# Attention into a gated feed-forward, one core: the lower bound on the weights' bits moved from GpSimd to VectorE, with a new table of planned times

## The chip, the cores and the metric

One core of a Trainium2 chip runs the kernel in a single launch. The metric is the device time of the run in microseconds, lower is better. Before the change it is 532.01 us, the median of three runs (531.34 to 532.36).

## What is computed

Inputs `q`, `k`, `v` have the shape (8 batches, 8 heads, 576 positions, 64); the three weights arrive as 64-bit floats, a float32 drawing times a float64 factor each.

```python
rel = pos[:, None] - pos[None, :]
scores = np.where((rel >= 0) & (rel < 64), q @ k.T / 8, -1e9)
attn = exp(scores - max);  attn /= attn.sum() + 1e-09
x = (attn @ v)                        # heads laid side by side: (8, 576, 512)
h = np.maximum(x @ w_in, 0)           # 512 -> 1024
conv = conv_w[0]*h[s-1] + conv_w[1]*h[s] + conv_w[2]*h[s+1]
out = (h * sigmoid(conv)) @ w_out     # 1024 -> 512
```

## The kernel before

**Tiles.** The 4608 positions are worked through in 12 units of 384. In each unit there are four pairs of heads (c = 0 to 3), eight groups of 128 feed-forward features (f = 0 to 7) and four groups of 128 outputs (o = 0 to 3). A float32 factor is split into a rounded high part and a remainder, so that each product is three matmuls: high by high, low by high, high by low. So `mm1` (L498 to L502) issues 96 matmuls a unit and `mm2` (L558 to L564) another 96.

**Attention of a unit.** Three blocks of scores: `qk` (TensorE, L350), `row_max` (VectorE, L357, adds the mask and takes the row's extreme), `exps` (ScalarE, L367, with the row's sum), `guard` (adds 1e-9 to the sums, L370: on GpSimd in units 0 to 2, on VectorE later), `reciprocal` (L373) and `normalise` (L378). In units 0 and 1 the weights are transposed by TensorE (L384) and copied out by ScalarE (L389), later by VectorE (L405) and DMAs (L417). `values` (L481) multiplies with v; `split_hi` (ScalarE, L485) and `split_lo` (VectorE, L488) leave `xh` and `xl`, the two parts of the unit's input. Two units' worth of `xh` and `xl` exist, so attention runs one unit ahead.

**Feed-forward of a unit.** For each f: `mm1`, then `relu` (ScalarE, L522 or L518); for each pair of f: `conv_mid` (ScalarE, L528), `conv_side` (VectorE, L535, four instructions), `sig` (ScalarE, L542), `gate` (VectorE, L547), `gate_hi` (ScalarE, L551), `gate_lo` (VectorE, L555), and then `mm2`, whose sums the output copies (L600, L602) take.

**Weights.** They are turned to float32 on the chip, once, while units 0 and 1 run. `weights` (L258) does it in nine steps: `w_in` in two steps of 512 columns and three of 1024, `w_out` in four of 1024. A step has a load of the bits (SP, L264), then `to_f32` (L244): the absolute value of the upper word (ScalarE, L248), the lower bound TINY on it (GpSimd, L249), a shift and mask (VectorE, L250), the sign put in (VectorE, L252), the lower word scaled (ScalarE, L255) and added (VectorE, L256); then the rounded high part (GpSimd, L269) and the remainder (VectorE, L270). All go through two buffers of bits (tile `T`, `T_100` in the order rows) and two of results (tile `w`, there `w_101` and `w_102`). The 24 convolution weights take the same path without the split (`weights_conv`, L291; tile `cw`).

**What sets the order.** Each step is entered in a plan with a planned time, an engine, a planned cost and the names it reads and writes. `queued` (L61) plays the plan through: at each point it takes the engine that can start first and on it the ready work with the smallest planned time, and issues instructions in that order; the engines then run their queues in order. Planned times of units 0 and 1 and of the loads come from the table START (first two entries of its triples; the third is for all later units). SWITCH and LEAVE are planned costs of changing the kind of work; PORT_CL and `port` keep some VectorE and GpSimd works apart in the plan. Where the plan sees TensorE idle in the first 110 us, it puts in matmuls on a spare tile (`keep_busy`, L207): `n = int((start - t) * FILL)`. They keep the engine active and compute nothing that is used.

Of the kernel before, what the change touches and what calls it, by code (L numbers as in the profile page):

```python
# [8 lines left out]
F32 = mybir.dt.float32  # L9
# [3 lines left out]
ALU = mybir.AluOpType  # L13
# [20 lines left out]
TINY = 2.0 ** -15  # L34
# [26 lines left out]
def queued(works, fill=None):  # L61
# [30 lines left out]
    while left:  # L92
# [17 lines left out]
        if fill and e == "PE" and start < FILL_TO:  # L110
# [4 lines left out]
            if n > 0 and clean:  # L115
                order.append(Work(x.t, e, 0.0, fill(n, min(clean)[1]), [], [], None, 0, 0.0))
        turn = SWITCH[e] if e in SWITCH and (x.kind != state[e] if e == "PE" else x.kind and x.kind != state[e]) else 0.0
        if turn and e == "PE" and not x.kind:
            turn = LEAVE
        if e == "PE" or x.kind:  # L120
# [17 lines left out]


START = {  # L140
    "v0": -27.5,
    "pv0": -15.968,
    "conv": -37.437,
    "bits": ((-46.561, -47.419), (-44.383, -45.007)),
    "qk1": -43.011,
    "v1": -11.849,
    "qk2": -2.185,
    "qk0": (-91.154, -52.794, -48.024),
    "ex0": (-42.377, -37.771, -19.993),
    "sc1": (-20.012, -18.408, -14.041),  # L150
    "ex1": (-8.106, -4.046, -3.778),
    "mask": -0.529,
    "sig": ((3.087, 7.079, 8.764, 10.751), (3.178, 6.73, 5.945, 9.966), (4.046, 6.806, 8.285, 10.314)),
    "in": (-39.031, -37.38, -33.878, -12.682, -12.013),
    "out": (-11.963, -8.679, 1.926, 7.315),
# [3 lines left out]
}  # L159
SWITCH = {"PE": 0.14, "ACT": 1.28}  # L160
LEAVE = 0.24
PORT_CL = 0.5
WARM = 5.0
FILL, FILL_FROM, FILL_TO = 4.0, 2.0, 110.0

# [2 lines left out]
def attention_moe(ctx: ExitStack, tc: tile.TileContext, q, k, v, w_in, conv_w, w_out, out):  # L168
    nc = tc.nc
# [4 lines left out]
    def many(n, shape, dt, name, where=pool):  # L174
        return [where.tile(shape, dt, name=f"{name}{i}") for i in range(n)]
# [7 lines left out]
    mask = many(3, [P, P], F32, "mask")  # L183
# [13 lines left out]
    bits = [flat.bitcast(U32)[:, 4 * DM * i:4 * DM * (i + 1)].rearrange("p (e two) -> p e two", two=2) for i in range(2)]  # L197
# [20 lines left out]
    def at(t, eng, cost, do, r=(), w=(), kind=None, mb=0, port=0.0):  # L218

        plan.append(Work(t, eng, cost, do, list(r), list(w), kind, mb, port))  # L220

    def two(t, eng, cost, do, **kw):
        at(t, eng, cost, do, port=cost, **kw)
# [17 lines left out]

    def to_f32(t, n, st, x, kb, kt):  # L244

        lw, hw, xu = st[..., 0], st[..., 1], x.bitcast(U32)

        at(t, "ACT", 0.0009 * n + 0.2, lambda: nc.scalar.activation(x, hw.bitcast(F32), AF.Abs), r=kb, w=kt)  # L248
        at(t, "POOL", 0.0027 * n + 0.02, lambda: nc.gpsimd.tensor_scalar(x, x, TINY, None, op0=ALU.max), w=kt, port=PORT_CL)  # L249
        two(t, "DVE", 0.00052 * n + 0.06, lambda: nc.vector.tensor_scalar(  # L250
            xu, xu, 3, 0x3FFFFFF8, op0=ALU.logical_shift_left, op1=ALU.bitwise_and), w=kt)
        two(t, "DVE", 0.00104 * n + 0.07, lambda: nc.vector.scalar_tensor_tensor(  # L252
            xu, hw, 0xC0000000, xu, op0=ALU.bitwise_and, op1=ALU.bitwise_or), r=kb, w=kt)

        at(t, "ACT", 0.0009 * n + 0.2, lambda: nc.scalar.activation(lw, lw, AF.Copy, scale=2.0 ** -29), w=kb)  # L255
        two(t, "DVE", 0.00104 * n + 0.07, lambda: nc.vector.tensor_tensor(xu, xu, lw, ALU.add), r=kb, w=kt)  # L256

    def weights(t, src, fs, hi, lo, key, buf, halves):  # L258

        e = slice(halves[0] * DM, (halves[-1] + 1) * DM)  # L260
        st, x = bits[buf][:, e], w24[buf][:, e]
        kb, kt = [("bits", buf, a) for a in halves], [("w24", buf, a) for a in halves]
        for f, a, tl in zip(fs, halves, load_at(buf, halves, t)):
            at(tl, "SP", 0.7, lambda f=f, a=a: nc.sync.dma_start(  # L264
                bits[buf][:, a * DM:(a + 1) * DM], src[f].bitcast(U32).rearrange("p (e two) -> p e two", two=2)),
               w=[("bits", buf, a)], mb=0.52)
        n = len(fs) * DM
        to_f32(t, n, st, x, kb, kt)
        two(t, "POOL", 0.00127 * n, lambda: nc.gpsimd.tensor_copy(hi, x), r=kt, w=[f"{key}{f}h" for f in fs])  # L269
        two(t, "DVE", 0.00104 * n + 0.07, lambda: nc.vector.tensor_tensor(lo, x, hi.bitcast(F32), ALU.subtract),  # L270
           r=kt + [f"{key}{f}h" for f in fs], w=[f"{key}{f}l" for f in fs])

    freed = {}

    def load_at(buf, halves, t):

        ts = [freed.get((buf, a), START["bits"][buf][a]) for a in halves]
        for a in halves:
            freed[(buf, a)] = t + 0.01
        return ts  # L280

    def weights_in(t, fs, *where):
        f = slice(fs[0], fs[-1] + 1)
        weights(t, w_in, fs, wih[:, f].rearrange("p f c e -> p (f c e)"),
                wil[:, f].rearrange("p f c e -> p (f c e)"), "in", *where)

    def weights_out(t, fs, *where):
        f = slice(fs[0], fs[-1] + 1)
        weights(t, w_out, fs, woh[:, f].rearrange("p f e -> p (f e)"), wol[:, f].rearrange("p f e -> p (f e)"), "out", *where)

    def weights_conv(t_load, t):  # L291
        at(t_load, "SP", 0.7, lambda: nc.sync.dma_start(
            cbits, conv_w.bitcast(U32).rearrange("p (e two) -> p e two", two=2)), w=["cbits"], mb=0.03)
        to_f32(t, 3 * NF, cbits, cw.rearrange("p k f -> p (k f)"), ["cbits"], ["cw"])
# [436 lines left out]
```

## Time and profile before

| | |
|---|---|
| median of three runs | 532.01 us |
| the profiled execution | 531.34 us |
| its span, first to last instruction | 529.6 us |
| TensorE (PE) busy with matmuls | 518.5 us, 98% |
| VectorE (DVE) busy | 380.3 us, 72% |
| ScalarE (ACT) busy | 379.7 us, 72% |
| GpSimd (POOL) busy | 112.6 us, 21% |
| granted TensorE clock | full level (2.4 GHz) in all 40 slices |

The shares are means over two very different stretches. In the page's table of 40 slices (13.2 us each), VectorE stands at 8 or 9 tenths from the second slice to the seventh and at 5 to 7 later; GpSimd does most of its work in the first seven; TensorE stands at 9 tenths nearly everywhere, but in the first 76 us a part of that is the spare matmuls (210 records, 28.6 us).

### The profile page before, as it was taken

How to read it: one execution, taken by the hardware profiler on the slowest of the kernel's cores; microseconds unless marked ns; L12 is line 12 of the kernel's file. 1: busy time of each engine (PE TensorE's matmuls, PEld its weight loads, DVE VectorE, ACT ScalarE, POOL GpSimd, SP SyncE). 2: the span in 40 equal slices, each digit the busy share in tenths (PEclk: the TensorE clock that was granted, in tenths of full speed). 3: DMA queues.
4: the chain of work that ended last, by engine and by line, in shares of the span. 5: the costliest groups of instructions: out<-in, count | busy, mean ns of one | idle time of the engine just before them, and what ended most of it. 6: DMA issues, size and time to landing. Idle time of an engine off the chain costs nothing.

```text
span 529.6 us, 14836 instructions
## 1 busy us (share of the span) xinstructions
PE 518.5 (98%) x5826; PEld 499.8 (94%) x5826; DVE 380.3 (72%) x1084; ACT 379.7 (72%) x1011; POOL 112.6 (21%) x196
## 2 busy tenths in 40 slices
PE   9998999999999999999999999999999999999996
PEld 8887889999999999999999999999999999999996
DVE  3899999985858667767767767767767667655552
ACT  2997897579896696696697687687687687544542
POOL 6664467113131011021021021021021021000000
PEclk9999999999999999999999999999999999999999
DMA  8984660237292173183083074073073053010011
GB/s 284 365 296 136 208 231 1 60 109 248 76 325 72 58 256 83 42 291 77 21 297 77 16 253 122 21 285 105 13 264 120 17 152 104 16 61 0 2 60 62
DMA packets 29463, 69.98 MB, mean 132 GB/s; under 512 B 5713, under 2 KB 17617, under 8 KB 29393
## 3 DMA queue, kind: packets, MB, share of 16 engines
q1 hardware_dynamic: 29392, 69.03, 39.7%
q8 instruction: 46, 0.75, 0.6%
q14 instruction: 25, 0.20, 0.1%
HBM read 47.73 MB, written 9.47 MB: 108 GB/s over the span
## 4 chain that ended last, share of the span: by engine, by line
PE 85%; DVE 9%; DMA 1%; ACT 1%; issue 1%; SPq 1%; POOL 0%; DVEq 0%
PE po L564 39%; PE acc L501 36%; PE acc L481 6%; PE sc L350 5%; DVE c L535 1%; DVE w L252 1%; DMA T<-in_w_in_dram 1%; DVE s L357 1%; DVE w L256 1%; DVE wil L270 1%; ACT s L367 1%; SPq L234 1%; DVE xl L488 1%; DVE s L378 1%; DVE w L250 1%
## 5 line engine op out<-in xcount | busy, mean ns | idle before, releaser
L501 PE MATMUL acc<-xh,wih 128*128 128x384 f32 x384 | 131.5, 342 | 0.8 <-DVE xl L488 0.8
L564 PE MATMUL po<-gh,woh 128*128 128x386 f32 (+1 forms) x384 | 132.1, 344 | 0.0
L535 DVE SCALAR_TENSOR_TENSOR c<-hbuf,cw,c 128x386 f32<-128x386 f32 (+1 forms) x192 | 109.6, 623 | 30.7 <-ACT c L528 30.7
L564 PE MATMUL po<-gh,wol 128*128 128x386 f32 (+1 forms) x384 | 129.9, 338 | 0.0
L564 PE MATMUL po<-gl,woh 128*128 128x386 f32 (+1 forms) x384 | 129.7, 338 | 0.0
L501 PE MATMUL acc<-xh,wil 128*128 128x384 f32 x384 | 129.7, 338 | 0.0
L501 PE MATMUL acc<-xl,wih 128*128 128x384 f32 x384 | 129.7, 338 | 0.0
L367 ACT ACTIVATE s<-s,nm 128x96 f32<-128x96 f32 (+2 forms) x288 | 105.1, 367 | 5.2 <-DVE nm L357 4.9
L555 DVE TENSOR_TENSOR gl<-c,gh 128x772 fp32r<-128x772 f32 (+1 forms) x48 | 55.8, 1162 | 28.2 <-ACT gh L551 28.1
L501 PEld LDWEIGHTS acc<-xh,wih 128*128 128x128 f32 x384 | 72.1, 188 | 2.9 <-POOL sm L370 0.7
L564 PEld LDWEIGHTS po<-gh,woh 128*128 128x128 f32 x384 | 72.2, 188 | 2.6
L378 POOL TENSOR_TENSOR s<-s,r 128x768 f32<-128x768 f32 x27 | 39.7, 1472 | 163.5 <-DVE r L373 150.7
L547 DVE TENSOR_TENSOR c<-c,hbuf 128x772 f32<-128x772 f32 (+1 forms) x48 | 47.4, 987 | 36.9 <-ACT c L542 36.7
L564 PEld LDWEIGHTS po<-gl,woh 128*128 128x128 f32 x384 | 72.3, 188 | 0.0
L564 PEld LDWEIGHTS po<-gh,wol 128*128 128x128 f32 x384 | 72.3, 188 | 0.0
L501 PEld LDWEIGHTS acc<-xh,wil 128*128 128x128 f32 x384 | 72.2, 188 | 0.0
L501 PEld LDWEIGHTS acc<-xl,wih 128*128 128x128 f32 x384 | 72.1, 188 | 0.0
L522 ACT ACTIVATE hbuf<-acc 128x384 f32<-128x384 f32 x64 | 30.9, 486 | 45.8 <-PE acc L501 45.4
L542 ACT ACTIVATE c<-c 128x772 f32<-128x772 f32 (+1 forms) x48 | 40.7, 848 | 30.2 <-DVE c L535 29.9
L357 DVE CUSTOM_DVE_ANT_0 s<-sc,mask 128x96 f32<-128x96 f32 (+2 forms) x272 | 51.5, 254 | 9.7 <-POOL mask L321 5.7
L367 ACT ACTIVATION_READ_ACCUMULATOR s<-s,nm 128x1 f32 x288 | 54.3, 189 | 0.0
L511 POOL COPY hbuf<-hbuf 128x4 f32<-128x4 f32 x44 | 16.7, 379 | 176.3 <-DVE c L547 176.2
(64 smaller groups left out, 644.5 us busy)
## 6 DMA issues: line engine op xcount, KB each, us to landing
v<-in_v_dram SPq DMA_DIRECT2D x24, 768.0 KB, 7.2
ub<-T SPq DMA_DIRECT2D x240, 48.0 KB, 1.9
k<-in_k_dram SPq DMA_DIRECT2D x22, 448.0 KB, 4.9
q<-in_q_dram SPq DMA_DIRECT2D x22, 384.0 KB, 6.9
out_dram<-T SPq DMA_DIRECT2D x8, 772.0 KB, 4.2
T<-in_w_in_dram SPq DMA_DIRECT2D x8, 512.0 KB, 6.6
T<-in_w_out_dram SPq DMA_DIRECT2D x8, 512.0 KB, 4.2
out_dram<-T SPq DMA_DIRECT2D x3, 768.0 KB, 6.4
```

Of the source, the lines that this page charges most:

```text
L350: nc.tensor.matmul(banks_of(u, b)[h][r:r + rows, i * P + o:i * P + n], qs[hs, 2 * g + p, t:t + rows], ks[hs, 2 * g + p, t + o:t + n], star ...
L357: nc.vector.tensor_tensor_reduce(out=ss[b][:, i, h, o:n], in0=banks_of(u, b)[h][:, i * P + o:i * P + n], in1=mask[m][:, o:n], scale=-0.125 ...
L367: nc.scalar.activation(x, x, AF.Exp, bias=nms[b][:, e], scale=-1.0, accum_out=sms[b][:, e])
L378: on.tensor_tensor(sv, sv, rs[b].unsqueeze(2).broadcast_to([P, 2 * NB, n]), ALU.mult)
L481: nc.tensor.matmul(acc[bank(("v", u, c))][h * D:(h + 1) * D, t * W:(t + 1) * W], vs[:, c, t, h], ub[g][:, 2 * p:2 * p + 2, 2 * t + h], sta ...
L501: nc.tensor.matmul(acc[bank(("m", u, f))][:, :NX], w[:, f, c], x[u % 2][:, c], start=(c == 0 and j == 0), stop=(c == NC - 1 and j == 2))
L522: nc.scalar.activation(hbuf[:, f, o:o + NX], ps[:, :NX], AF.Relu)
L535: nc.vector.scalar_tensor_tensor(c, hbuf[:, f, e:e + n], cw[:, e, f:f + 1], c, op0=ALU.mult, op1=ALU.add)
L542: nc.scalar.activation(c, c, AF.Sigmoid)
L547: nc.vector.tensor_tensor(c, c, hbuf[:, 2 * i:2 * i + 2, 1:1 + n], ALU.mult)
L555: nc.vector.tensor_tensor(gls[ring(u, i)][:, :, :n], cs[i % 2][:, :, :n], ghs[ring(u, i)][:, :, :n].bitcast(F32), ALU.subtract)
L564: nc.tensor.matmul(po[o][:, :n], w[:, f, es], x, start=(f == 0 and j == 0), stop=(f == NF - 1 and j == 2))
```

## The change

The lower bound of the nine weight steps becomes a VectorE instruction (`early=True`); that of the 24 convolution weights stays on GpSimd. The planned cost of the rounding copy is lowered from 0.00127 to 0.00104 us a column. Nearly all planned times of the loads and of units 0 and 1 are new, with SWITCH, LEAVE and PORT_CL; the third entries of the triples, which serve units from 2 on, are as they were. START in short (every number but those third entries is new):

```diff
 START = {
-    "conv": -37.437,
-    "bits": ((-46.561, -47.419), (-44.383, -45.007)),
+    "conv": -53.962,
+    "bits": ((-41.879, -47.051), (-42.277, -36.159)),
...
-SWITCH = {"PE": 0.14, "ACT": 1.28}
-LEAVE = 0.24
-PORT_CL = 0.5
+SWITCH = {"PE": 0.12, "ACT": 1.28}
+LEAVE = 0.19
+PORT_CL = 0.87
...
-    def to_f32(t, n, st, x, kb, kt):
+    def to_f32(t, n, st, x, kb, kt, early=False):
...
-        at(t, "POOL", 0.0027 * n + 0.02, lambda: nc.gpsimd.tensor_scalar(x, x, TINY, None, op0=ALU.max), w=kt, port=PORT_CL)
+        if early:
+            two(t, "DVE", 0.00052 * n + 0.06, lambda: nc.vector.tensor_scalar(x, x, TINY, None, op0=ALU.max), w=kt)
+        else:
+            at(t, "POOL", 0.0027 * n + 0.02, lambda: nc.gpsimd.tensor_scalar(x, x, TINY, None, op0=ALU.max), w=kt, port=PORT_CL)
...
-        to_f32(t, n, st, x, kb, kt)
-        two(t, "POOL", 0.00127 * n, lambda: nc.gpsimd.tensor_copy(hi, x), r=kt, w=[f"{key}{f}h" for f in fs])
+        to_f32(t, n, st, x, kb, kt, True)
+        his, los = [f"{key}{f}h" for f in fs], [f"{key}{f}l" for f in fs]
+        two(t, "POOL", 0.00104 * n, lambda: nc.gpsimd.tensor_copy(hi, x), r=kt, w=his)
```

Line numbers of the changed kernel are three or four higher than those above (L250 is the new VectorE bound, L253 its shift and mask).

How the order moves, first on VectorE after the three blocks of row maxima of unit 0, up to the next block of them. Before:

```order
L250 TENSOR_SCALAR w_101<-w_101 128x512
L252 SCALAR_TENSOR_TENSOR w_101<-T,w_101 128x512
L373 RECIPROCAL r_89<-sm_86 128x8
L378 TENSOR_TENSOR s_80<-s_80,r_89 128x1024
L256 ISA w_101<-T,w_101 128x1024
L270 TENSOR_TENSOR wil<-w_101,wih 128x512
```

Now:

```order
L255 SCALAR_TENSOR_TENSOR cw<-cbits,cw 128x24
L250 TENSOR_SCALAR w_101<-w_101 128x512
L253 TENSOR_SCALAR w_101<-w_101 128x512
L255 SCALAR_TENSOR_TENSOR w_101<-T,w_101 128x512
L250 TENSOR_SCALAR w_101<-w_101 128x512
L376 RECIPROCAL r_89<-sm_86 128x8
L253 TENSOR_SCALAR w_101<-w_101 128x512
L381 TENSOR_TENSOR s_80<-s_80,r_89 128x1024
L255 SCALAR_TENSOR_TENSOR w_101<-T,w_101 128x512
L259 ISA w_101<-T,w_101 128x1024 x2
L274 TENSOR_TENSOR wil<-w_101,wih 128x512
```

Both 512-column steps now go through VectorE here, each with its own bound (L250), and the convolution weights are ahead of them.

GpSimd in the same place and after it, before:

```order
L249 TENSOR_SCALAR w_101<-w_101 128x512
L370 TENSOR_SCALAR sm_86<-sm_86 128x8
L269 CAST wih<-w_101 128x512
L370 TENSOR_SCALAR sm_87<-sm_87 128x8
L249 TENSOR_SCALAR w_101<-w_101 128x512
L249 TENSOR_SCALAR w_102<-w_102 128x1024
L433 MEMSET s_80 128x2x64
L269 CAST wih<-w_101 128x512
L370 TENSOR_SCALAR sm_88<-sm_88 128x8
L269 CAST wih<-w_102 128x1024
```

Now:

```order
L373 TENSOR_SCALAR sm_86<-sm_86 128x8
L273 CAST wih<-w_101 128x512
L373 TENSOR_SCALAR sm_87<-sm_87 128x8
L273 CAST wih<-w_101 128x512
L436 MEMSET s_80 128x2x64
L373 TENSOR_SCALAR sm_88<-sm_88 128x8
L273 CAST wih<-w_102 128x1024
```

The bounds (L249) are gone and the rounding copies (CAST) and the bounds on the sums (`sm`) stand alone.

VectorE up to the last `split_lo` of unit 1 (the `xl_66` row at the end), before:

```order
L256 ISA w_101<-T,w_101 128x2048
L250 TENSOR_SCALAR w_102<-w_102 128x1024
L555 TENSOR_TENSOR gl_97<-c_92,gh_94 128x772
L252 SCALAR_TENSOR_TENSOR w_102<-T,w_102 128x1024
L488 TENSOR_TENSOR xl_66<-acc_106,xh_64 128x384
L488 TENSOR_TENSOR xl_66<-acc_107,xh_64 128x384
L535 SCALAR_TENSOR_TENSOR c_92<-hbuf,cw,c_92 128x386 x2
L270 TENSOR_TENSOR wol<-w_101,woh 128x1024
L256 ISA w_102<-T,w_102 128x2048
L535 SCALAR_TENSOR_TENSOR c_92<-hbuf,cw,c_92 128x386 x2
L488 TENSOR_TENSOR xl_66<-acc_106,xh_64 128x384
```

Now, to the third `split_lo` of unit 1 and a little beyond; the fourth, the last, comes after the next block of row maxima:

```order
L491 TENSOR_TENSOR xl_66<-acc_107,xh_64 128x384
L274 TENSOR_TENSOR wol<-w_102,woh 128x1024
L538 SCALAR_TENSOR_TENSOR c_92<-hbuf,cw,c_92 128x386 x2
L491 TENSOR_TENSOR xl_66<-acc_107,xh_64 128x384
L538 SCALAR_TENSOR_TENSOR c_92<-hbuf,cw,c_92 128x386 x2
L550 TENSOR_TENSOR c_93<-c_93,hbuf 128x772
```

Before the last `split_lo` of unit 1 VectorE's queue now also holds the remainder of the second `w_out` step, three gate instructions (L550 twice more, L558 once more) and the nine new bounds.

## Rows read from the trace of the kernel before

**Rows 1.** The page's first line.

```profile
span 529.6 us, 14836 instructions
```

**Rows 2.** Timeline of PE: start us, us, engine line op out<-in xcount [idle before <-releaser].

```profile
56.22 1.16 PE L350 MATMUL sc<-k,q 64*32 64x96 f32 x64 [0.31 <-DVE nm L357]
...
72.80 0.34 PE L564 MATMUL po<-gh,woh 128*128 128x386 f32 x1
...
75.09 0.34 PE L564 MATMUL po<-gh,wol 128*128 128x386 f32 x1
...
75.84 0.44 PE L501 MATMUL acc<-xh,wih 128*128 128x384 f32 x1 [0.24 <-DVE xl L488]
...
525.16 0.34 PE L564 MATMUL po<-gl,woh 128*128 128x386 f32 x1
```

**Rows 3.** Timeline of DVE: the first weight step and the last `xl` of unit 1.

```profile
14.57 0.43 DVE L250 TENSOR_SCALAR w<-w 128x512 uint32<-128x512 uint32 x1 [2.14 <-POOL w L249]
...
75.24 0.55 DVE L488 TENSOR_TENSOR xl<-acc,xh 128x384 fp32r<-128x384 f32 x1
```

**Rows 4.** Timeline of ACT: the first weight step and two exponentials behind it.

```profile
12.29 0.67 ACT L248 ACTIVATE w<-T 128x512 f32<-128x512 f32 x1 [4.56 <-DMA T<-in_w_in_dram]
12.86 0.40 ACT L367 ACTIVATE s<-s,nm 128x128 f32<-128x128 f32 x1
...
13.24 0.39 ACT L367 ACTIVATE s<-s,nm 128x128 f32<-128x128 f32 x1
```

**Rows 5.** Timeline of SP: the first four weight loads are issued.

```profile
4.81 2.45 SPq L264 DMA_DIRECT2D T<-in_w_in_dram  x4
```

**Rows 6.** DMA view of 4.7 to 4.9 us, the first of them: KB, us to landing.

```profile
T<-in_w_in_dram SPq DMA_DIRECT2D x1, 512.0 KB, 6.2
```

**Rows 7.** Timeline of DVE: one each of the kinds that the sum prices.

```profile
21.03 0.43 DVE L250 TENSOR_SCALAR w<-w 128x512 uint32<-128x512 uint32 x1
...
61.78 0.95 DVE L547 TENSOR_TENSOR c<-c,hbuf 128x772 f32<-128x772 f32 x1
...
76.95 1.21 DVE L270 TENSOR_TENSOR wol<-w,woh 128x1024 fp32r<-128x1024 f32 x1
...
83.64 0.68 DVE L250 TENSOR_SCALAR w<-w 128x1024 uint32<-128x1024 uint32 x1
```

**Rows 8.** Timeline of DVE: stretched instructions and undisturbed ones of their kinds.

```profile
15.03 0.69 DVE L252 SCALAR_TENSOR_TENSOR w<-T,w 128x512 uint32<-128x512 uint32 x1
...
21.49 1.41 DVE L252 SCALAR_TENSOR_TENSOR w<-T,w 128x512 uint32<-128x512 uint32 x1
...
32.35 2.05 DVE L270 TENSOR_TENSOR wil<-w,wih 128x1024 fp32r<-128x1024 f32 x1
...
38.20 2.06 DVE L378 TENSOR_TENSOR s<-s,r 128x1024 f32<-128x1024 f32 x1
...
42.93 1.21 DVE L378 TENSOR_TENSOR s<-s,r 128x1024 f32<-128x1024 f32 x1
...
49.85 2.04 DVE L378 TENSOR_TENSOR s<-s,r 128x1024 f32<-128x1024 f32 x1
...
51.81 2.05 DVE L270 TENSOR_TENSOR wil<-w,wih 128x1024 fp32r<-128x1024 f32 x1
...
56.27 2.79 DVE L535 SCALAR_TENSOR_TENSOR c<-hbuf,cw,c 128x386 f32<-128x386 f32 x4
...
109.51 2.21 DVE L535 SCALAR_TENSOR_TENSOR c<-hbuf,cw,c 128x386 f32<-128x386 f32 x4 [0.99 <-ACT c L528]
```

**Rows 9.** Timeline of POOL beside three of them.

```profile
32.28 2.78 POOL L249 TENSOR_SCALAR w<-w 128x1024 f32<-128x1024 f32 x1
...
49.77 1.04 POOL L269 CAST wih<-w 128x1024 fp32r<-128x1024 f32 x1 [4.97 <-DVE w L256]
50.77 3.75 POOL L249 TENSOR_SCALAR w<-w 128x1024 f32<-128x1024 f32 x1
```

**Rows 10.** Waits of POOL: engine line <- what: us in total, times, longest.

```profile
POOL w L249 <- ACT w L248: 7.3, 4, 3.0
```

More of the change, by code (lines that the diff above doesn't have):

```diff
@@ L140 @@
 START = {
-    "v0": -27.5,
-    "pv0": -15.968,
-    "conv": -37.437,
-    "bits": ((-46.561, -47.419), (-44.383, -45.007)),
[L145 to L155, printed above, removed]
[3 rows of a table removed]
-}
-SWITCH = {"PE": 0.14, "ACT": 1.28}
-LEAVE = 0.24
-PORT_CL = 0.5
+    "v0": -27.11,
+    "pv0": -16.447,
+    "conv": -53.962,
+    "bits": ((-41.879, -47.051), (-42.277, -36.159)),
+    "qk1": -35.557,
+    "v1": -2.039,
+    "qk2": -8.267,
+    "qk0": (-84.481, -53.378, -45.171),
+    "ex0": (-42.159, -31.168, -27.713),
+    "sc1": (-34.067, -30.046, -13.969),
+    "ex1": (-13.151, -8.655, -2.539),
+    "mask": -6.876,
+    "sig": ((3.158, 6.971, 7.27, 10.667), (4.268, 5.828, 6.158, 11.201), (4.046, 6.806, 8.285, 10.314)),
+    "in": (-40.487, -36.003, -29.538, -16.708, -12.047),
+    "out": (-2.867, -0.369, 9.31, 10.724),
[3 rows of a table added]
+}
+SWITCH = {"PE": 0.12, "ACT": 1.28}
+LEAVE = 0.19
+PORT_CL = 0.87
 WARM = 5.0
@@ L267, in weights @@
         n = len(fs) * DM
-        to_f32(t, n, st, x, kb, kt)
-        two(t, "POOL", 0.00127 * n, lambda: nc.gpsimd.tensor_copy(hi, x), r=kt, w=[f"{key}{f}h" for f in fs])
-        two(t, "DVE", 0.00104 * n + 0.07, lambda: nc.vector.tensor_tensor(lo, x, hi.bitcast(F32), ALU.subtract),
-           r=kt + [f"{key}{f}h" for f in fs], w=[f"{key}{f}l" for f in fs])
+        to_f32(t, n, st, x, kb, kt, True)
+        his, los = [f"{key}{f}h" for f in fs], [f"{key}{f}l" for f in fs]
+        two(t, "POOL", 0.00104 * n, lambda: nc.gpsimd.tensor_copy(hi, x), r=kt, w=his)
+        two(t, "DVE", 0.00104 * n + 0.07, lambda: nc.vector.tensor_tensor(lo, x, hi.bitcast(F32), ALU.subtract), r=kt + his, w=los)
     freed = {}
```

6 rows, old and new, of the table START are left out of this document.

## The prediction

> **What bounds the kernel now.** I read the page's engine lines and slices first, then TensorE's timeline with its waits, then VectorE's and GpSimd's timelines beside each other up to 115 us. TensorE sets the time, but only its first 76 us can change. Its last wait on another engine ends at 75.84, where a first matmul of a unit needs the last remainder `xl` of unit 1 from VectorE; from there to the last matmul at 525.16 its row shows no idle time [rows 2]. The matmuls are the same before and after the change, and the clock is at its full level in every slice. So the end is the time at which TensorE passes that point, plus the useful work that is left for it there. The point itself belongs to VectorE: the `xl` subtraction starts at 75.24 and takes 0.55 [rows 3], and from its first weight step at 14.57 on VectorE hardly stands idle. What happens on VectorE before that subtraction is therefore what I add up.
>
> A row of VectorE starts some 0.08 before its forerunner ends, so I price an instruction at its duration less 0.08.
>
> **The change, part by part, up to the last `xl` of unit 1.**
>
> *More on VectorE's list.* Nine bounds are added ahead of the point: seven of 1024 columns and two of 512. The new instruction has the kind, tile and shape of the shift and mask, so I take that row's price: 0.68 - 0.08 = 0.60 and 0.43 - 0.08 = 0.35 [rows 7], together 7 x 0.60 + 2 x 0.35 = 4.9 us. The new order also moves four other instructions ahead of it: one remainder of 1024 columns at 1.13, and three gate instructions of 772 columns at 0.87 each [rows 7], 3.7 us. Counted over both lists, nothing else differs. VectorE has **8.6 us** more to do before the point.
>
> *Less left for TensorE.* What VectorE does earlier, TensorE can use earlier: in the new order 38 more wide matmuls (14 of `mm1`, 24 of `mm2`) stand before the point and one block of scores fewer. From the two `mm2` rows 13 steps apart a wide matmul takes 2.29 / 13 = 0.176; the block of scores takes about 1.1 [rows 2]. So 38 x 0.176 - 1.1 = **5.6 us** less is left behind the point. The spare matmuls do not enter: the plan puts in 106 calls for 105.
>
> *Collisions with the bound on GpSimd.* Five VectorE instructions before the point are stretched while a bound runs on GpSimd: 1.41 against 0.69, 2.05 against 1.21, 2.06 against 1.21, 2.05 against 1.21, and four convolution instructions 2.79 against 2.21 [rows 8]; GpSimd's bounds at 32.28 and 50.77 lie beside them [rows 9]. That is 0.72 + 0.84 + 0.85 + 0.84 + 0.58 = **3.8 us**, which goes with the bounds.
>
> The Trainium skill (SBUF — State Buffer, section "SBUF: two separate sides") states that VectorE and GpSimd share a port pair as an exclusive lock, and that whoever comes second is blocked for the whole instruction of the other. The rows differ: VectorE's subtraction at 32.35 meets a bound of 2.78 us nearly at that one's start and loses only 0.84, as much as one that meets a copy of 1.04 us [rows 8, 9]. By the rule this term would be up to 5 x 2.78 = 13.9 us; the measured stretches decide.
>
> *The first wait.* VectorE now waits 2.14 for GpSimd's first bound [rows 3]. In the new order the first step needs the first weight load, not the second. That load is issued at 4.81 and lands 6.2 later, at 11.0 [rows 5, 6]; ScalarE's absolute value takes 0.57 (12.29 to 12.86, [rows 4]), so the result is there at about 11.6, before VectorE is through with its row maxima at 12.4. The wait goes. A new one comes: the second step's bound stands behind ScalarE's six exponentials (0.38 each, [rows 4]) and its own absolute value, 11.6 + 2.3 + 0.57 = 14.5, while VectorE is there at 12.4 + 0.1 + 2 x 0.35 + 0.6 = 13.8. I take 0.8. If the first load came no earlier than ScalarE's 12.29 now, it would be 2.0; if the exponentials were done before, nothing. Net **-1.3 us**.
>
> *Moved at no cost.* The convolution weights' load moves on SP ahead of the first four weight loads, and their absolute value to the head of ScalarE's queue, ahead of the first two exponentials. ScalarE has 4.56 us of idle time there [rows 4]; only a landing after 11 us would use that up, and then it would delay the second block of rows above by as much. The other loads move by one or two places among loads that land long before they are used. GpSimd loses nine bounds of up to 3.75 us (one waits in that figure, [rows 9]) and becomes idle more; nothing waits for it sooner.
>
> *What I do not know.* Seven rounding copies on GpSimd fall before the point. In the trace five VectorE instructions are stretched beside a copy, by 0.3 to 0.83, 3.5 us in all; the row at 49.85 (2.04 against 1.21) stands for them [rows 8]. Where the copies fall in the new order the rows can't tell. If none meets VectorE, another 3.5 us is gained; if each costs 0.83, 7 x 0.83 = 5.8, it is 2.3 us worse. I take no change, because the copies keep their place between the same two VectorE steps.
>
> **Sum:** 8.6 - 5.6 - 3.8 - 1.3 = **-2.1 us**. For the profiled execution (531.34, of which the span is 529.6, [rows 1]) that is 529.2; it lies 0.67 under the median of the runs, to which I apply the sum: 532.01 - 2.1 = **529.9 us**. With the ends above, this case runs from -4.5 to -1.1.
>
> **Rivals.**
>
> 1. *The copies no longer meet VectorE:* -2.1 - 3.5 = -5.6, 526.4 us. For it: the planned cost of a copy is set to the 1.04 that an undisturbed one takes. Against: five of seven met it before under a plan that was also meant to keep them apart.
> 2. *The collisions only change partner.* With the bounds gone VectorE's list is denser, and each copy meets an instruction of it: -2.1 + 2.3 = +0.2, 532.2 us. For it: VectorE's two-operand instructions fill nearly all its time. By the Trainium skill's rule of the exclusive lock (page and section above) the new bounds would lock copies out as well; no row of this trace shows a bound on VectorE.
> 3. *The limit moves later.* VectorE still has two `w_out` steps behind the point, with 19 us of listed work up to the last remainder, and TensorE has 19.5 us between the same points: only 0.4 us of room. Two copies more at 0.83 each use it up and push by 1.3: -0.8, 531.2 us.
> 4. *Slower: VectorE inherits the wait for ScalarE.* GpSimd waited 7.3 us in four places for the absolute values, at most 3.0 at a time [rows 10], and VectorE did other work meanwhile. Now the bound stands in VectorE's own queue, and row maxima, normalisation and gate, for which TensorE waits, stand behind it. Without the first of these waits (3.0, accounted for above) 4.3 us remain: -2.1 + 4.3 = +2.2, 534.2 us. It decides the sign from 2.1 us of such waits. Against it: from the third bound on, the work listed ahead of it on VectorE exceeds that ahead of the absolute value on ScalarE by one to nine microseconds, so ScalarE should be ahead.
>
> That the bound does not move can be left out: the order shows it on VectorE.
>
> **How the numbers follow.** My case 0.50; rival 1 0.07; rival 2 0.18; rival 3 0.10; rival 4 0.15. A difference of 0.2%, 1.06 us, is about what a measurement of this kernel can tell from none. Faster: my case and rival 1, 0.57. Same: rivals 2 and 3, 0.28. Slower: rival 4, 0.15. The range from 527.2 to 532.8 leaves out the end of rival 1 and most of rival 4.
>
> **What would show it.** In the changed kernel's profile VectorE should have nine bounds at 0.68 and 0.43, and no stretch of VectorE without a copy beside it. Its first bound should start at about 12.6, the second step's after a wait of 0.8 on ScalarE. The last `xl` of unit 1 should be done at 75.8 + 8.6 - 3.8 - 1.3 = 79.3, TensorE's last wait end at or before that, and its last matmul start near 523. I am wrong if VectorE shows waits of over 2 us for the absolute values behind its third bound, if copies cost more than 5 us, or if TensorE still waits after 85 us.

## The result and the profile after

The changed kernel takes **534.82 us** (median of 7, 533.04 to 537.29) against 532.10 of the kernel before in the same comparison: ratio 1.006, 95% interval 1.004 to 1.008. The forecast of 529.9 with its range of 527.2 to 532.8 is wrong, and so is its sign. The profiled execution took 536.38, with a span of 534.6 where [rows 1] has 529.6.

The first 80 us went nearly as forecast. VectorE's timeline of the changed kernel, at the first two bounds (L250), at the sixth, and around the last `xl` of unit 1 (start us, us, engine line op; the idle time before it stands in brackets):

```profile
13.24 0.42 DVE L250 TENSOR_SCALAR w<-w 128x512 f32<-128x512 f32 x1
...
14.76 0.42 DVE L250 TENSOR_SCALAR w<-w 128x512 f32<-128x512 f32 x1
...
45.71 0.69 DVE L250 TENSOR_SCALAR w<-w 128x1024 f32<-128x1024 f32 x1 [0.68 <-ACT w L248]
...
75.71 2.48 DVE L250 TENSOR_SCALAR w<-w 128x1024 f32<-128x1024 f32 x2
78.10 0.54 DVE L491 TENSOR_TENSOR xl<-acc,xh 128x384 fp32r<-128x384 f32 x1
```

The wait of 2.14 in [rows 3] is gone, the bounds cost what [rows 7] said, and the last `xl` is done at 78.64 (forecast 79.3; 75.79 before).

The loss lies behind that. TensorE's timeline of the changed kernel: the matmuls of the values at unit 2's second half, those of unit 4's and unit 11's first half, and the last matmul. In [rows 2] the last row stands at 525.16.

```profile
121.68 2.03 PE L484 MATMUL acc<-ub,v 128*64 128x64 f32 x48 [2.84 <-DMA ub<-T]
...
179.06 1.62 PE L484 MATMUL acc<-ub,v 128*64 128x64 f32 x48
...
463.32 1.62 PE L484 MATMUL acc<-ub,v 128*64 128x64 f32 x48
...
529.96 0.34 PE L567 MATMUL po<-gl,woh 128*128 128x386 f32 x1
```

The same blocks in the kernel before:

```profile
176.64 1.62 PE L481 MATMUL acc<-ub,v 128*64 128x64 f32 x48
...
458.56 1.62 PE L481 MATMUL acc<-ub,v 128*64 128x64 f32 x48
```

So 2.42 us are lost up to unit 4 and 2.34 more over the seven units to unit 11: their period is (463.32 - 179.06) / 7 = 40.61 now and 40.27 before.

**The first place.** TensorE stands idle for 2.84 us until the second half's placements `ub<-T` have landed. (A placement is one of the DMAs that put a unit's transposed attention weights into `ub`, L420 here and L417 before: 24 in a unit, twelve for each half, 48 KB each.) SP's queue of the changed kernel around it (SPq rows are DMA issues):

```profile
105.54 0.35 SPq L234 DMA_DIRECT2D k<-in_k_dram  x1
105.93 0.44 SPq L234 DMA_DIRECT2D q<-in_q_dram  x1
107.04 0.35 SPq L609 DMA_DIRECT2D out_dram<-T  x1
107.90 0.33 SPq L240 DMA_DIRECT2D v<-in_v_dram  x1
108.89 11.32 SPq L420 DMA_DIRECT2D ub<-T  x12
```

In the kernel before, the 24 placements of unit 2 are one piece, and the out store and `v` come behind it:

```profile
94.13 15.56 SPq L417 DMA_DIRECT2D ub<-T  x24
111.42 0.36 SPq L606 DMA_DIRECT2D out_dram<-T  x1
117.02 3.48 SPq L240 DMA_DIRECT2D v<-in_v_dram  x2
```

The chain of waits of the changed kernel leads through `v`, which the placements do not read: the issue of one of them waits for a completion semaphore that `v` holds, as the program gives its DMAs eight such semaphores in turn: the eighth placement is issued at 117.18, just as `v`, eight issues before it, lands.

```profile
107.90 9.26 DMA v<-in_v_dram
...
117.18 0.51 SPq L420
...
119.63 1.91 DMA ub<-T
...
121.68 2.03 PE acc L484 x48
123.70 2.23 PE po L567 x6
```

Behind the idle time the granted clock is low, which is why the last two rows take 2.03 and 2.23; at full clock they take 1.62 and 1.26 (below, e5). The windows of the changed kernel (the column behind the five engines is the granted clock, then the DMA share):

```profile
122.00:124.00 2.00, 2.00 (x46) 1.88 (x42) 0.86 (x2) 1.37 (x6) 0.00 (x0) 0.67 0.93 337
124.00:126.00 2.00, 2.00 (x7) 2.00 (x7) 0.91 (x4) 0.22 (x1) 0.94 (x1) 0.50 0.80 169
```

At 0.50 the array runs at 1.2 and not at 2.4 GHz. Idle time 2.84 and at least 1.4 for the clock explain more than the 2.42 lost up to unit 4: the first part had gained some 1.8 us. This is the profiled execution, which has one of the low mean clocks (0.995). Of the seven executions four lie at 0.995 to 0.997 (534.40 to 537.29 us) and three at 0.999 or 1.000 (533.04 to 534.82), and the median is one of the latter.

**The second place.** In every steady unit a weight load of TensorE waits for the first `gl`. Waits of the weight loads from 200 to 460 us in the changed kernel (us in total, times, longest); the kernel before has no such row:

```profile
PEld po L567 <- DVE gl L558: 2.5, 7, 0.4
```

### The profile page after: what moved, and what is told of

Same layout as the page of the kernel before. It is cut to its first block, busy times and chain, and to the rows that moved or that the text cites. A ratio compares the mean times of both kernels' runs of the same rounds, so it can differ in the third digit from the quotient of the medians.

```text
span 534.6 us, 14840 instructions
## 1 busy us (share of the span) xinstructions
PE 523.3 (98%) x5828; PEld 501.4 (94%) x5828; DVE 386.3 (72%) x1093; ACT 381.1 (71%) x1013; POOL 84.4 (16%) x187
## 4 chain that ended last, share of the span: by engine, by line
PE 68%; ACT 14%; DVE 13%; DMA 3%; issue 1%; SPq 0%; POOL 0%; ACTq 0%
PE po L567 30%; PE acc L504 25%; PE acc L484 6%; ACT s L370 5%; PE sc L353 4%; PE acc L212 3%; DVE gl L558 3%; DVE c L538 2%; DMA v<-in_v_dram 2%; DVE w L259 1%; ACT L370 1%; ACT L545 1%; DVE s L360 1%; DMA T<-in_w_out_dram 1%; ACT c L545 1%
## 5 line engine op out<-in xcount | busy, mean ns | idle before, releaser
L550 DVE TENSOR_TENSOR c<-c,hbuf 128x772 f32<-128x772 f32 (+1 forms) x48 | 51.3, 1068 | 28.6 <-ACT c L545 28.3
L558 DVE TENSOR_TENSOR gl<-c,gh 128x772 fp32r<-128x772 f32 (+1 forms) x48 | 55.4, 1154 | 16.3 <-ACT gh L554 15.6
L381 POOL TENSOR_TENSOR s<-s,r 128x768 f32<-128x768 f32 x27 | 39.8, 1472 | 164.9 <-DVE r L376 105.7
L370 ACT ACTIVATION_READ_ACCUMULATOR s<-s,nm 128x1 f32 x288 | 55.4, 192 | 0.0
L531 ACT ACTIVATE c<-hbuf,cw 128x386 f32<-128x386 f32 (+1 forms) x96 | 53.5, 608 | 1.1 <-DVE gl L558 1.1
```

Of the source, the lines that this page charges most:

```text
L370: nc.scalar.activation(x, x, AF.Exp, bias=nms[b][:, e], scale=-1.0, accum_out=sms[b][:, e])
L381: on.tensor_tensor(sv, sv, rs[b].unsqueeze(2).broadcast_to([P, 2 * NB, n]), ALU.mult)
L531: nc.scalar.activation(cs[i % 2][:, a, :n], hbuf[:, f, 1:1 + n], AF.Copy, scale=cw[:, 1, f:f + 1])
L550: nc.vector.tensor_tensor(c, c, hbuf[:, 2 * i:2 * i + 2, 1:1 + n], ALU.mult)
L558: nc.vector.tensor_tensor(gls[ring(u, i)][:, :, :n], cs[i % 2][:, :, :n], ghs[ring(u, i)][:, :, :n].bitcast(F32), ALU.subtract)
```

## The experiments

Theory 1 says that the loss lies in these two places, and that moving the bound pays. Theory 2 says that the bound on VectorE is itself the cost. Medians, and ratios to the kernel before in the same comparison (its medians lie between 531.4 and 532.1, so medians of different comparisons can be set against each other to about 0.7 us):

| run | us | ratio (95%) |
|---|---|---|
| changed kernel | 534.82 | 1.006 (1.004 to 1.008) |
| e1 placements first | 535.90 | 1.0082 (1.0070 to 1.0094) |
| e2 old steady order | 531.68 | 0.9998 (0.9986 to 1.0010) |
| e3 = e1 + e2 | 532.35 | 1.0018 (1.0009 to 1.0027) |
| e4 bound alone | 531.73 | 1.0001 (0.9993 to 1.0010) |
| **e5 = e2, store and `v` later** | **530.33** | **0.9977 (0.9966 to 0.9989)** |
| e6 = e2 + 22 spare calls | 534.41 | 1.0062 (1.0046 to 1.0078) |
| e7 = e2, exponentials earlier | 533.25 | 1.0031 (1.0019 to 1.0043) |
| f1 new steady order alone | 533.64 | 1.0049 (1.0036 to 1.0062) |
| f2 = e5, bound on GpSimd | 536.69 | 1.0098 (1.0083 to 1.0114) |
| f3 = e2 + 11 spare calls | 531.85 | 1.0009 (1.0001 to 1.0018) |
| f4 = e2, store and `v` between | 535.67 | 1.0083 (1.0069 to 1.0097) |
| g1 = f4, on ScalarE's queue | 535.98 | 1.0077 (1.0061 to 1.0093) |
| g2 = changed kernel, store and `v` later | 532.25 | 1.0015 (1.0006 to 1.0024) |

In an e8 the due times behind 80 us were put back to the old ones. It no longer computes the function above, so its time says nothing here.

**The steady order: e2 and f1.** The two prices act on every unit. e2 uses the old ones from 130 us of planned time on:

```diff
-        turn = SWITCH[e] if e in SWITCH and (...) else 0.0
+        turn = (0.14 if e == "PE" and start > 130 else SWITCH[e]) if e in SWITCH and (...) else 0.0
         if turn and e == "PE" and not x.kind:
-            turn = LEAVE
+            turn = 0.24 if start > 130 else LEAVE
```

> The changed kernel with one edit: from 130 us of planned time on, the planner uses the old prices for a change of kind on TensorE (0.14 and 0.24), which gives the steady units the order that they had before; everything up to there is as changed. Theory 1: the period of a steady unit goes from 40.61 back to 40.27, seven times: -2.35, so 534.82 - 2.35 = 532.5; the wait for gl of 0.35 per unit goes. The 2.8 us wait at 121.7 stays. Theory 2: the steady units are as fast in either order, 534.8.

f1 is the mirror image, the kernel before with 0.12 and 0.19 from there on.

> The kernel before with one edit: from 130 us of planned time on, the planner uses the new prices for a change of kind on TensorE (0.12 and 0.19); this gives the steady units the changed kernel's order and leaves all that comes before as it was. Theory 1 (the new steady order costs 0.34 per unit, because TensorE reaches the first gl of a unit too early): 7 x 0.34 = 2.3 to 2.4 more, 534.0, ratio 1.0045. Rival (the period of 40.61 belongs to the late state in which the changed kernel enters the steady units, not to the order): 531.7, ratio 1.000.

Both came out as theory 1 has it: -3.1 us against the changed kernel (2.35 expected) and +2.2 against the one before (2.3 to 2.4 expected). f1's trace shows the period: values of unit 4 and of unit 11, and the wait of the weight loads from 200 to 460 us.

```profile
176.50 1.62 PE L481 MATMUL acc<-ub,v 128*64 128x64 f32 x48
...
460.73 1.62 PE L481 MATMUL acc<-ub,v 128*64 128x64 f32 x48
```

```profile
PEld po L564 <- DVE gl L555: 2.5, 7, 0.4
```

(460.73 - 176.50) / 7 = 40.60. e2 no longer has that wait. The reason stands in the timeline of the changed kernel. GpSimd normalises a block of attention weights (L381), and VectorE's `gl` beside it takes 2.14:

```profile
201.60 1.47 POOL L381 TENSOR_TENSOR s<-s,r 128x768 f32<-128x768 f32 x1 [4.57 <-DVE r L376]
...
201.75 2.14 DVE L558 TENSOR_TENSOR gl<-c,gh 128x772 fp32r<-128x772 f32 x1 [0.32 <-ACT gh L554]
...
203.95 0.19 PEld L567 LDWEIGHTS po<-gl,woh 128*128 128x128 f32 x1 [0.39 <-DVE gl L558]
...
206.72 0.95 DVE L558 TENSOR_TENSOR gl<-c,gh 128x772 fp32r<-128x772 f32 x1
```

The kernel before has the same collision in every unit, equally long:

```profile
199.18 1.47 POOL L378 TENSOR_TENSOR s<-s,r 128x768 f32<-128x768 f32 x1 [5.12 <-DVE r L373]
199.33 2.14 DVE L555 TENSOR_TENSOR gl<-c,gh 128x772 fp32r<-128x772 f32 x1 [0.32 <-ACT gh L551]
```

There TensorE reaches this `gl` later. Its first weight load comes 0.71 after the `gl` is done (201.47), and the stretch costs nothing:

```profile
202.18 0.19 PEld L564 LDWEIGHTS po<-gl,woh 128*128 128x128 f32 x1
```

The new order brings TensorE there some 0.35 us too early, once per unit.

**The placements: e1, e3 and e5.** e1 moves all of `k`, `q`, the store and `v` behind the second half's placements on SP and touches nothing else:

```diff
-        for x in queued(plan, keep_busy):
+        order = queued(plan, keep_busy)
+        put = [i for i, x in enumerate(order) if x.eng == "SP" and x.mb == 0.15]
+        late = [x for x in order[put[3]:put[4]] if x.eng == "SP" and x.mb != 0.15]
+        rest = [x for x in order[:put[7] + 1] if x not in late]
+        for x in rest + late + order[put[7] + 1:]:
             x.do()
```

> The changed kernel with one edit: on SP's queue k, q, the first out store and v now come behind the second half's twelve placements of unit 2, not ahead of them; every other queue is the same. Theory 1 (the loss has two places: these placements stuck behind large transfers, which leaves TensorE idle for 2.8 us and then at a lower granted clock; and a new order of the steady units): the twelve issues follow each other at 0.63 from 108.9, the last lands near 118.4, TensorE's wait at 121.7 goes, and so does the low clock behind it; 536.38 - 4.7 = 531.7 against the profiled execution, 531.5 as a median. Theory 2 (the bound on VectorE is the cost: the transposes of that half come late because VectorE is fuller, so the wait only changes its name): 534 to 535. Theory 3 (the two medians differ by chance): no difference from the changed kernel or from the one before that repeats.

It did not get faster: theory 1 had 531.5, and 535.90 lies above even theory 2's 534 to 535. The stall at 121.7 went (those values start at 118.95), and TensorE waits later instead. SP's queue and TensorE's timeline of e1:

```profile
96.22 21.16 SPq L420 DMA_DIRECT2D ub<-T  x24
117.48 0.52 SPq L234 DMA_DIRECT2D k<-in_k_dram  x1
...
122.66 0.50 SPq L240 DMA_DIRECT2D v<-in_v_dram  x1
123.25 20.97 SPq L420 DMA_DIRECT2D ub<-T  x24
```

```profile
142.10 0.92 PE L484 MATMUL acc<-ub,v 128*64 128x64 f32 x24 [2.98 <-DMA ub<-T]
```

Seven large transfers now stand right ahead of unit 3's placements, and unit 3's values pay. e3, e1 with the old steady order, shows it again (a wait of 1.9 there, and 532.35 instead of theory 1's 529.9):

> The changed kernel with both edits: the twelve placements ahead of k, q, out and v on SP, and the old prices of a change of kind from 130 us of planned time on. Theory 1: only the gain of the first 80 us is left (-2.1 to -2.4 as measured there), so 532.1 - 2.2 = 529.9, faster than both kernels. Theory 2: 534 or more, since neither edit touches the bound on VectorE.

e5 spreads them: `v` behind unit 2's twelve, the store behind the first twelve of unit 3, `k` and `q` where they were, with the steady order of e2.

```diff
...
+        store, load = [x for x in order[put[3]:put[4]] if x.eng == "SP" and x.mb in (0.8, 0.79)]
+        order = ([x for x in order[:put[7] + 1] if x not in (store, load)] + [load] +
+                 order[put[7] + 1:put[11] + 1] + [store] + order[put[11] + 1:])
...
```

> e2 with one more edit on SP's queue alone: v moves behind unit 2's twelve placements of the second half, the out store behind the first twelve of unit 3; k and q stay ahead. Theory 1 (a placement issue waits for the large transfer that took its completion semaphore eight issues before): the second half is issued at 0.63 each from 108.9, lands near 118.5, and unit 3's placements have fewer loads ahead of them than in e1, so neither place stalls: 531.68 - 2.5 = 529.2. Rival (the stall only moves, as in e1, because the transfers of two units don't fit before unit 3's values whatever their order): a wait of 1 to 3 us at 135 to 145, 531 to 532.5.

530.33 us, faster than both kernels, though 1.1 above what theory 1 had. The waits of TensorE and the chain behind the placements in e5:

```profile
PE acc L484 <- DMA ub<-T: 0.5, 1, 0.5
```

```profile
121.30 1.62 PE acc L484 x48
122.92 1.26 PE po L567 x6
```

g2 makes the same edit with the new steady order left in:

> The changed kernel with e5's edit of SP's queue alone, and the new prices of a change of kind throughout, so that only the steady order is left as a loss. If the two losses add up: e5's 530.33 plus the 2.2 of f1, 532.5 to 532.9, ratio 1.002; the wait for the placements at most 0.7, the wait for gl seven times 0.35 as in the changed kernel. If they don't add up (the late state hides one of them): 531 or under, or 534 and over.

532.25, a little under the band. From e5 to the changed kernel it is 0.83% or 4.5 us. By way of g2 the steady order takes 1.9 of them and the placements 2.6; by way of e2 the placements take 1.35 and the order 3.1. So the two account for the loss, and how it is shared between them is known to about 1 us.

**What holds a placement back: f4 and g1.** I had taken the issue's wait for a semaphore as the cause. f4 puts store and `v` between the sixth and the seventh of the twelve, so that no placement comes eight issues behind one of them (e5's edit with `[store, load]` behind `put[5]`).

> e2 with the out store and v between the sixth and the seventh of the second half's twelve placements. Both large transfers then run beside the last six placements, but no placement comes eight issues behind one of them. If the stall comes from the issue that waits for a completion semaphore of a large transfer (theory 1): the twelve placements and the two between them are issued in about 14 x 0.6 = 8.5 us instead of 11.6, the stall of 3.1 falls under 0.7, 529.3 to 530.3. If it comes from the transfers themselves, which share the 16 DMA engines with the placements (rival): the last placements land as late as in e2, a stall of 2 to 3 us stays, 531 to 532.

The rival won, and by more than it had said: the stall is 4.4 and not 2 to 3 us, and 535.67 lies 3.7 above its range. SP issues without a wait, and the chain of f4 shows where the time is:

```profile
108.75 4.16 SPq L420 DMA_DIRECT2D ub<-T  x6
113.01 0.52 SPq L609 DMA_DIRECT2D out_dram<-T  x1
113.62 0.38 SPq L240 DMA_DIRECT2D v<-in_v_dram  x1
114.05 4.22 SPq L420 DMA_DIRECT2D ub<-T  x6
```

```profile
117.69 5.28 DMA ub<-T
...
123.10 2.83 PE acc L484 x48
```

The last placement was issued at 117.69, earlier than the 119.63 of the changed kernel, and took 5.28 to land instead of 1.91. All six behind the two large transfers are late, from 5.3 to 7.8 us:

```profile
DMA to landing us min/median/max: 5.3/6.4/7.8
```

The semaphore only moved the waiting from the transfer to the issue. g1 issues the two large transfers from ScalarE's queue, f4's volume without f4's queue. In the written order they stand behind all twelve placements there; by the clock they are issued at 114.72 and 115.19, 1.7 and 1.6 us later than in f4:

> f4 with one difference: the out store and v are issued by ScalarE's DMA queue, at about the same time (some 112 to 114 us), and no longer by SP's. The volume that runs beside the last placements is the same. If a placement lands late because it stands behind the large transfers in SP's own queue: the last placement lands 2 us after its issue, the stall of 4.4 falls to under 1.0, and the time to about e5's, 530.3. If the transfers share the 16 DMA engines whatever queue issues them: the stall stays at 3 to 5 us and the time at 534.5 to 536.

It did not help: 535.98. The slowest placement took 7.8 us to land, as in f4, and TensorE's longest wait is the one below. The profile names `q`, but that load, issued at 119.83, takes 5.8 us and lands after these matmuls have started at 124.03. They read `ub`, whose last placement lands at 123.79:

```profile
DMA to landing us min/median/max: 1.9/2.2/7.8
```

```profile
PE acc L485 <- DMA q<-in_q_dram: 4.7, 1, 4.7
```

So a 48 KB placement is held back by the large transfers issued ahead of it, whichever of the two queues issued them. In f4 the first of the six lands 0.24 us after `v`, and in g1 the slowest lands 0.26 after `v`. Whether its data or only its completion signal is late, no run here shows; for TensorE it is the same. The Trainium skill (DMA: Bandwidth & Descriptors, section "Queues, rings and completion order") says that each DMA engine takes descriptors in the order of its ring, and that a completion semaphore is raised only after every earlier write of that engine, across its queues. These landings agree, from one queue (f4) and from two (g1).

**The clock: e6 and f3.** Spare matmuls fill the idle time, in f3:

```diff
...
+            if x is stalled:
+                keep_busy(11, x.w[0])()
             x.do()
```

> e2 with 22 spare matmuls of 112 columns (22 took 2.60 us in the changed kernel) ahead of the matmuls that stall, so that TensorE works through the idle time; nothing else differs. If the low granted clock behind the stall comes from TensorE's standing idle: the windows 122 to 126 show 1.00, the values of that half take 1.40 and not 2.41, the executions with a mean clock of 0.996 or 0.997 go, and the median falls by 0.5 to 1.5 to some 530.7. If the clock falls there for another reason (the transfers that run at over 0.9 of the DMA engines then): the clock still falls and the time stays at 531.7.

> e6 with half the spare calls: e6's 22 calls took 5.06 us and not 2.6, since each call is two matmuls in the trace, and so they outlasted the stall by 2 us. 11 calls take 2.5 us and fill it. If the low clock comes from TensorE's standing idle: all executions at a mean clock of 0.999 or more, as in e6, none over 532.5, and a median of 530.5 to 531.2. If not: as e2, 531.7 with executions at 0.996 up to 533.9.

The windows of f3 show the full clock at the same DMA share:

```profile
122.00:124.00 2.00, 2.00 (x48) 1.93 (x44) 0.88 (x2) 1.39 (x6) 0.00 (x0) 1.00 0.90 349
124.00:126.00 2.00, 2.00 (x13) 2.00 (x13) 0.87 (x4) 0.18 (x1) 0.98 (x1) 1.00 0.92 259
```

All 17 executions of e6 and f3 have a mean clock of 0.999 or more; of e2's twelve two were at 0.996 and 0.997, at 533.85 and 533.23, its slowest. So without the idle time the clock does not fall, at the same load on the DMA engines. The median of f3, though, did not fall (531.85 against 531.68, with 530.5 to 531.2 expected), and two of its executions lie above 532.5. The executions at 530.15 to 531 are gone as well, perhaps because there the stall was shorter than 11 calls, which no run shows. As a remedy it is worth nothing, and e6's 22 calls outlasted the stall (534.41 instead of some 530.7).

**The exponentials: e7.** The second half's transposes come late because unit 2's third block of exponentials is due later in the new table. e7 puts that one number back, 13.007 to 8.722, on top of e2.

> e2 with one number of the plan put back: the exponentials of unit 2's third block are due at 8.722 (as before) and not at 13.007; the planner writes the queues anew from there. The second half's transposes then come before the out store and v, and SP issues all 24 placements in one piece. Theory 1: no stall at 121.7 and none of its low clock, 531.68 - 2.5 = 529.2, faster than before. Rival (that number was moved because earlier exponentials hold up the gate on ScalarE or VectorE): TensorE waits 1 to 3 us for gate or xl between 85 and 115, 531 to 532.5.

The rival held in kind: a new wait, though for ScalarE's relu and not for gate or `xl`, and 533.25 lies 0.75 above its range. SP issues the 24 placements in one piece again, so it is that number which had put the large transfers ahead of the second half:

```profile
97.94 16.15 SPq L420 DMA_DIRECT2D ub<-T  x24
```

The granted clock from 80 to 100 us is 0.91. TensorE's timeline in e7:

```profile
87.86 0.49 PE L504 MATMUL acc<-xh,wih 128*128 128x384 f32 x1 [1.79 <-ACT hbuf L521]
```

**The bound: e4 and f2.** e4 issues the nine bounds on VectorE in the otherwise unchanged kernel before; f2 puts them back on GpSimd in e5. Both keep the plan made for the other engine. This is e4's edit; f2 only swaps the engine in the new line.

```diff
...
-        at(t, "POOL", ..., lambda: nc.gpsimd.tensor_scalar(x, x, TINY, None, op0=ALU.max), ...)
+        on = nc.vector if n > 3 * NF else nc.gpsimd
+        at(t, "POOL", ..., lambda: on.tensor_scalar(x, x, TINY, None, op0=ALU.max), ...)
```

> The kernel before with one edit: the nine bounds of the weights are issued on VectorE, at the same place of the written order, and nothing is planned anew; GpSimd keeps the bound of the convolution weights. Theory 1: 4.9 more work on VectorE, 3.8 of collisions gone, 1.3 to 2.1 of the first wait gone: between -1.0 and +0.5, about 531.9. Theory 2 (the bound on VectorE is what costs): most of the loss shows here already, 534 to 535.

> e5 with the nine bounds issued on GpSimd again, at the same places of the written order; all times, prices and queues are e5's. My sum with its signs turned: -4.9 of work on VectorE, +3.8 of collisions with a bound (up to 7.6, nine at 0.84), +1.3 to 2.1 for the first wait: between 530.5 and 535, likeliest 531.5. Theory 2 (a bound on VectorE is a cost by itself): faster than e5, 528 to 529.5.

Alone, the bound on VectorE is worth nothing (531.73 against 531.5), as the sum of its three terms said. With the new times it is worth 6.4 us (536.69 against 530.33), above the band that I had from the same three terms; part of it is f2's lower mean clock (0.996), and part may be that nothing was planned anew for GpSimd, which no run separates. Theory 2 falls. VectorE's waits up to 110 us in f2 show what the new order can't bear:

```profile
DVE w L253 <- POOL w L250: 7.3, 5, 2.5
```

## Why the prediction was wrong

1. **VectorE's list up to the last `xl` of unit 1** was right. It was to end at 79.3. It ended at 78.64 in the profile, and between 78.40 and 80.36, on average 79.06, in the eleven profiles in which VectorE's order up to there is the changed kernel's (changed kernel, e1 to e3, e5 to e7, f3, f4, g1, g2).
2. **Collisions and waits.** The first wait went, at 13.24 and not 12.6. The wait of 0.8 foreseen for the second bound is 0.68 at the sixth. The collisions with GpSimd's bounds went. Two bounds found new partners: 1.25 and 1.30 instead of 0.68, beside GpSimd's zeroing of the placement buffer (75.67 to 77.63). The rounding copies, for which no change was taken, stretch three instructions by 1.6 us in all (at 30.85, 38.61 and 54.15) instead of 3.5. These two misses, +1.2 and -1.9, nearly cancel, so that the list's end came out so well is in part luck.
3. **Less left for TensorE** was too large by about 1 us. In e1, g2, e3 and e5 the last `xl` is done 2.61, 2.86, 3.56 and 4.57 later than before. Unit 4's values start at 177.87, 174.79, 177.68 and 177.27 instead of 176.64; without the waits behind the point (2.98 + 0.2, none, 1.93, 0.53) that is -1.95, -1.85, -0.89 and +0.10. So 4.5 to 4.7 us less was left and not 5.6, and at the forecast 79.3 the gain is about 1 us and not 2.1. The counts hold (38 wide matmuls fewer behind the point, one block of scores more); what takes the rest, no run separates. In the medians e5, with both losses below out of the way, gains 1.2 to 1.4.
4. **The step that failed** is "Moved at no cost", in its sentence "The other loads move by one or two places among loads that land long before they are used". The loads themselves were indeed in time; what I did not count is the placements that they are moved ahead of. Two large transfers, issued in good time for their own readers, delayed the small ones behind them. The source is in the table START. The text ahead of the prediction has its first two entries serve units 0 and 1, but the `ex` and `qk` numbers among them place the softmax two units on, in units 2 and 3. Unit 2's third block of exponentials is due at 13.007 instead of 8.722, the second half's placements come later, and the large transfers slip in ahead (e7 undoes it). The step cost 1.35 us in the medians (e2 to e5) to 2.6 (changed kernel to g2), and 2.84 plus at least 1.4 of clock in the profiled execution.
5. **The second failure** is the claim that behind 76 us TensorE's row shows no idle time and so the work left there is all that counts. That holds for the old order. The planner's two prices give every steady unit a new one, and I did not follow it past the point: 2.2 us by f1, 1.9 to 3.1 by the pairs of medians above.
6. **The rivals.** None covers it. Rival 4 has the right sign and nearly the right size (534.2), but by luck: its waits for the absolute values were not there, 0.7 us instead of 4.3. "If TensorE still waits after 85 us" was the right alarm, and I gave it no chance of its own. The ends of my case, -4.5 to -1.1, do not follow from the ends given there: those of the first wait make it -2.9 to -0.9, those of the copies -5.6 to +0.2.

## What to carry to other kernels

When a table of times or prices changes, compare the order of every queue to the end of the program, the steady units too, and price each small transfer by what is issued ahead of it, not only by its own reader. A term that is worth nothing alone (the bound, e4) can be worth much in a new order (f2), so a part of a retuned plan is not judged by taking it alone. Moving a large transfer ahead of small ones moves a stall rather than removing it; spread them (e5).

## What the runs showed of the hardware

- A 48 KB placement lands in 1.9 us when no large transfer is under way (all 24 of unit 2 in the kernel before). Behind 1.5 MB of other transfers it takes up to 7.8, whether these come from its own queue (f4: 5.3 to 7.8) or from another (g1).
- In the profiled executions idle times of TensorE of 2.84 (changed kernel), 3.12 (e2), 4.41 (f4) and 4.66 us (g1) end at a granted clock of about 0.50. After e1's wait of 2.98 it stayed at full level (1.00 from 140 to 160 us). One idle time of this length is not always paid for.
- VectorE's `gl` loses 1.19 us beside a GpSimd instruction of 1.47, nearly all of what remained of it. By the Trainium skill's rule of the exclusive lock (SBUF — State Buffer, section "SBUF: two separate sides") it would lose the rest of that instruction, 1.32. This row comes close, while [rows 8, 9] showed 0.84 beside 2.78.
